# Pooling keys of batch 0 and values of batch 1 on TensorE, with the first zeroing on VectorE

## The chip, the cores and the metric

The kernel runs on one core of one Trainium2 chip. The time of a run is what the device takes from start to end, in microseconds (us). Five engines work side by side, each through its own instructions in order: TensorE (PE: matrix products and transposes), VectorE (DVE), ScalarE (ACT), GpSimd (POOL) and SyncE (SP), which here issues all transfers between the device's memory and the core's (DMA). An engine that waits for a result of another stands still, and all that is queued behind it waits too.

## What is computed

```python
def _attn_ref(q, k, v):                  # q, k, v: 8 x 8 x 576 x 64
    k_p = k.reshape(B, H, Sp, pool, D).mean(axis=3)     # pool = 8, Sp = 72
    v_p = v.reshape(B, H, Sp, pool, D).mean(axis=3)
    scores = scale * np.matmul(q, k_p.transpose(0, 1, 3, 2))
    attn = softmax(scores)
    return np.matmul(attn, v_p)
...
x = attn_out                             # 4608 tokens x 512
x = (relu(x @ w_in) ** 2) @ w_out        # 512 -> 2048 -> 512
out = (sigmoid(x @ w_gate) * (x @ w_val)) @ w_out2      # 512 -> 1536 -> 512
```

Each attention head looks at 72 pooled keys and values instead of 576. The two feed-forward layers that follow are nearly all of the arithmetic.

## The kernel before

The 4608 tokens are cut into 12 blocks of 384 (`NA`). A block goes through attention in two halves of four heads (`attend`), then through the first layer (`expert1`): for each of 16 slices f of the hidden width, twelve matmuls make h (line 818), ScalarE and VectorE make g = relu(h)^2 and split it into an upper and a lower part (`ghi`, `glo`, line 874), and twelve matmuls add g times `w_out` to the block's sums (line 827). The first block is done in two parts with the second between them, so that the weights are needed later. The second layer follows in a second stage, after about 980 us.

The products are made from two-part numbers: each weight and each activation is split into an upper part of short mantissa and the rest, and three of the four products are added. A weight must therefore be converted before its first use (`convert`, `split`): a transfer brings it into a raw tile, GpSimd adds a constant (`round24`, line 236), ScalarE takes the absolute value (line 242), VectorE does four steps (lines 246, 249, 252, 257), ScalarE makes the upper part (line 273) and VectorE the lower (line 277, into `in` or `out`). All 32 weight slices are converted while the first two blocks run.

Keys and values are pooled in two ways. On VectorE: a sum over eight neighbours (`tensor_reduce`), line 627 for the keys of batch 0, two heads at a time (`early_keys`), and line 379 for the others, head by head (`prep`). On TensorE: `early_kv` loads all heads of one batch in three transfers of 128, 128 and 32 partitions, each partition with two neighbouring rows, and multiplies by the matrix `pm`, whose ones add up the rows that belong together (`pool_rows`, line 659). ScalarE copies the sum out. For keys TensorE then transposes the heads in pairs (line 697), and ScalarE puts them into `kpT`, from which the scores are made (line 441). `early_kv` is used for the values of batch 0 and the keys of batch 1. `pm` is made on VectorE (lines 357, 358) from the identity `ident`, which GpSimd makes in `constants`; there GpSimd also zeroes the two `kpT` and two `e_sb` tiles (line 354).

The order of all this isn't written out. `Plan` holds every operation with its engine, an estimated duration in us, a rank (its due time), its dependences and the buffers that it takes and gives. `Plan.run` plays the program through with these durations: at each moment an engine that is free takes the operation of least rank among those that are ready and whose buffers are free. The sequence that comes out is the order in which each engine gets its instructions. So a changed duration or rank can change the order anywhere, and the engines then run that order, whatever the true durations are.

Of the kernel before, what the change touches and what calls it, by code (L numbers as in the profile page):

```python
# [131 lines left out]
def kernel(  # L132
# [53 lines left out]
    V0L = 1.0  # L186
# [8 lines left out]
    n = 0  # L195
# [31 lines left out]
    def convert(src, rank, at, get_raw, raw_name, get_t, t_name, done, load_rank=None):  # L227
# [37 lines left out]
        for fn, d in ((b1, 0.36), (b2, 0.36), (b3, 0.62)):  # L265
            o = op("dve", d, fn, (o,), rank)
        o = op("dve", 0.62, b4, (o,), rank, give=(raw_name,))
        return done(s, o)

    def split(s, o, rank, get_slot, take, give, key):  # L270
# [11 lines left out]
        return op("dve", 0.63, lo, (o,), rank, give=give)  # L282
# [68 lines left out]
    def constants():  # L351
        make_identity(nc, ident)
        for t in kpT + e_sb:
            nc.gpsimd.memset(t, 0.0)

    def constants2():
        nc.vector.memset(pm, 0.0)
# [13 lines left out]
    def prep(be, hf, rank):  # L371
# [24 lines left out]
        for pr in range(2 if be > 1 else 0):  # L396
            ds = []
            for j in range(2):
                h = 4 * hf + 2 * pr + j
                o = op("dma", 0.5, lambda h=h: load(k, h), rank=rank, at=rank - 20, take=("kv",), lag=2.0)  # L400
                ds.append(op("dve", 0.6, lambda pr=pr, j=j, h=h: red_k(pr, j, h), (o,) + tuple(ds), rank,
# [4 lines left out]
        for h in range(4 * hf, 4 * hf + 4):  # L406
# [8 lines left out]
            v_ready[be, h] = op("dve", 0.6, red_v, [o] + prev + first, rank + 3, give=("kv",))  # L415
# [143 lines left out]
    def attend(b, hf, rank, step, q_ops, fast, bank_of):  # L559
# [3 lines left out]
        for a in range(NTA):  # L563
# [28 lines left out]
            else:  # L592
                late.append(op("dve", 0.47, lambda a=a: a_trans(b, hf, a), [o] + late[-1:], r + 4,
# [22 lines left out]

    def early_keys(n, rank):
        tiles, st = {}, {}
        for i in range(KT):
            def ld(i=i):  # L620
                tiles[i] = t = wpool.tile([SP, 2, POOL, D], F32, tag=w1_tag(n + i), name="rows8")
                nc.sync.dma_start(
                    out=t, in_=k[0, 2 * i:2 * i + 2].rearrange("h (n r) d -> n h r d", r=POOL))

            def red(i=i):
                st[i] = att.tile([SP, 2, D], F32, tag="kp", name="kp", bufs=2)
                nc.vector.tensor_reduce(
                    out=st[i], in_=tiles[i].rearrange("n h r d -> n h d r"), op=ALU.add, axis=AX.X)

            def tr(i=i):  # L630
                st["ps", i] = p = ps("acc3", 1)
                nc.tensor.transpose(p[:, 0:SP], st[i].rearrange("n j d -> n (j d)"), ident[0:SP, 0:SP])

            def place(i=i):
                for j in range(2):
                    nc.scalar.activation(
                        out=kpT[0][64 * j:64 * j + 64, i, j * SP:(j + 1) * SP],
                        in_=st["ps", i][64 * j:64 * j + 64, 0:SP], func=ACTF.Copy)
# [148 lines left out]
    for hf in range(2):  # L787
        prep(1, hf, t1 - P1 + A1 * hf)
# [636 lines left out]
```

## Time and profile before

| what | us |
|---|---|
| median of 3 runs | 1813.4 (1811.69 to 1816.31) |
| the profiled execution | 1808.99 |
| its span, first to last instruction | 1807.2 |
| TensorE busy | 1750.7 (97%) |
| VectorE busy | 1167.3 (65%) |
| ScalarE busy | 774.9 (43%) |
| GpSimd busy | 243.9 (13%) |

The profile is of one execution, and all rows quoted here are of that one; it lies 4.4 us under the median. Busy shares are means over the whole span, in which the stages differ; a stage is read from its own stretch. Where a row ends in square brackets, they hold the time that the engine was idle before it and what ended the wait.

### The profile page before, as it was taken

Reading aid. Unit: us, or ns where it says so; the run is one execution under the profiler, and the core shown is the slowest. Engines: PE = TensorE matmul, PEld = TensorE weight load, DVE = VectorE, ACT = ScalarE, POOL = GpSimd, SP = SyncE. Lnnn points to the kernel's source line nnn. Section 1 sums busy time; section 2 is a strip of 40 time slices with the busy share of each in tenths; the row PEclk is TensorE's granted clock in tenths of the full one; section 3 lists DMA queues with packets and bytes.
Section 4 is the critical chain, followed back from the end, with each engine's and each line's share of the span. In section 5 each row is a group of like instructions: output and inputs, shape, how many; then the busy total and the mean of one; then the engine's idle time right before and its main releaser. Section 6 shows DMA issues by size and latency. Waiting matters only on the chain.

```text
span 1807.2 us, 26430 instructions
## 1 busy us (share of the span) xinstructions
PE 1750.7 (97%) x9696; PEld 1636.6 (91%) x9696; DVE 1167.3 (65%) x2318; ACT 774.9 (43%) x1722; POOL 243.9 (13%) x190
## 2 busy tenths in 40 slices
PE   5899999999999999999999999999999999999999
PEld 2688889999899888999999999999999999999998
DVE  6999787778767776664246555555655655655554
ACT  4766533333333333233245444444444444444442
POOL 3400000000000000000013211212111211211100
PEclk9999999999999999999999999999999999999999
DMA  9732344433343333320112222223433333333321
GB/s 246 238 94 71 82 110 106 123 105 102 91 99 102 113 99 98 81 79 24 52 53 94 70 71 70 82 71 105 132 99 113 114 108 114 109 106 105 105 80 50
DMA packets 191250, 179.15 MB, mean 99 GB/s; under 512 B 105232, under 2 KB 139024, under 8 KB 191120
## 3 DMA queue, kind: packets, MB, share of 16 engines
q1 hardware_dynamic: 191120, 177.46, 33.1%
q8 instruction: 76, 1.25, 0.3%
q14 instruction: 54, 0.44, 0.1%
HBM read 119.80 MB, written 48.76 MB: 93 GB/s over the span
## 4 chain that ended last, share of the span: by engine, by line
PE 61%; DVE 2%; SPq 1%; DMA 1%; issue 0%; ACT 0%; POOL 0%; DVEq 0%; POOLq 0%; ACTq 0%
PE h L1208 16%; PE acc L1323 16%; PE att L1208 8%; PE acc L827 8%; PE h L818 7%; PE acc L1208 4%; SPq L518 1%; PE att L542 0%; PE att L441 0%; DVE kp L379 0%; DVE g L874 0%; DMA aT<-T 0%; DMA raw<-in_moe_w_val_dram 0%; DMA kv<-in_k_dram 0%; DVE r L867 0%
## 5 line engine op out<-in xcount | busy, mean ns | idle before, releaser
L827 PE MATMUL acc<-g,out 128*128 128x384 f32 x2304 | 447.9, 340 | 17.4 <-DVE g L874 9.4
L818 PE MATMUL h<-x,in 128*128 128x384 f32 x2304 | 439.5, 339 | 2.3 <-DVE x L812 1.3
L827 PEld LDWEIGHTS acc<-g,out 128*128 128x128 f32 x2304 | 399.7, 188 | 39.5 <-DVE g L874 19.3
L818 PEld LDWEIGHTS h<-x,in 128*128 128x128 f32 x2304 | 403.0, 189 | 10.1 <-issue 6.2
L861 ACT ACTIVATE r<-h 128x384 f32<-128x384 f32 x192 | 93.8, 489 | 232.7 <-PE h L818 229.3
L1323 PE MATMUL acc<-in,p 128*128 128x512 f32 x648 | 182.5, 390 | 0.0
L1323 PE MATMUL acc<-out,p 128*128 128x512 f32 x648 | 182.1, 389 | 0.0
L1230 ACT ACTIVATE res<-h 128x384 f32<-128x384 f32 x144 | 70.6, 491 | 211.7 <-PE h L1208 210.9
L871 ACT ACTIVATE g<-r 128x384 fp32r<-128x384 f32 x192 | 100.8, 525 | 138.7 <-DVE r L867 131.4
L867 DVE TENSOR_TENSOR r<-r,h 128x384 f32<-128x384 f32 x160 | 87.7, 548 | 111.8 <-ACT r L861 111.6
L1323 PEld LDWEIGHTS acc<-out,p 128*128 128x128 f32 x648 | 121.7, 188 | 25.7
L874 DVE TENSOR_TENSOR g<-r,g 128x384 fp32r<-128x384 f32 x192 | 112.3, 585 | 50.4 <-ACT g L871 49.9
L1323 PEld LDWEIGHTS acc<-in,p 128*128 128x128 f32 x648 | 121.4, 188 | 24.1
L236 POOL INT64_ADD raw<-raw x40 | 43.7, 1092 | 658.5 <-DMA raw<-in_moe_w_out_dram 278.8
L1239 DVE TENSOR_TENSOR res<-res,acc 128x384 f32<-128x384 f32 x72 | 39.7, 551 | 125.3 <-PE acc L1208 125.3
L1349 DVE TENSOR_TENSOR o<-o,acc 128x512 f32<-128x512 f32 x72 | 49.5, 687 | 96.0 <-PE acc L1323 81.2
L1289 ACT ACTIVATE p<-res 128x384 fp32r<-128x384 f32 x144 | 75.3, 523 | 70.5 <-DVE res L1283 70.3
L1041 POOL TENSOR_TENSOR yt<-yf,yt 128x768 f32<-128x768 f32 x32 | 62.2, 1944 | 270.8 <-DVE out L1068 269.6
L1208 PE MATMUL h<-out,in 128*128 128x384 f32 x432 | 98.4, 335 | 0.0
L1208 PE MATMUL h<-in,out 128*128 128x384 f32 x432 | 98.1, 334 | 0.2 <-DVE res L1239 0.2
L1208 PE MATMUL h<-in,in 128*128 128x384 f32 x432 | 98.1, 334 | 0.0
L1208 PE MATMUL h<-out,out 128*128 128x384 f32 x432 | 98.0, 334 | 0.0
(146 smaller groups left out, 2646.2 us busy)
## 6 DMA issues: line engine op xcount, KB each, us to landing
yf<-y_dram SPq DMA_DIRECT2D x16, 1536.0 KB
o_part<-o SPq DMA_DIRECT2D x72, 256.0 KB
o<-o_part SPq DMA_DIRECT2D x72, 256.0 KB
y_dram<-y SPq DMA_DIRECT2D x48, 192.0 KB
w_dram<-t SPq DMA_DIRECT2D x36, 256.0 KB
w2s<-w_dram SPq DMA_DIRECT2D x36, 256.0 KB
out_dram<-o SPq DMA_DIRECT2D x36, 256.0 KB
kv<-in_v_dram SPq DMA_DIRECT2D x56, 144.0 KB
```

The lines of the kernel that those rows point to most:

```text
L818: nc.tensor.matmul(out=h[:, 0:n], lhsT=w[:, a, kk * 128:(kk + 1) * 128], rhs=xs[kk][:, c], start=(kk == 0 and i == 0), stop=(kk == KT - 1 ...
L827: nc.tensor.matmul(out=y_ps[m][:, 0:NA], lhsT=w[:, a, m * 128:(m + 1) * 128], rhs=g_t[f][:, c], start=(f == f0 and i == 0), stop=(f == f1 ...
L861: nc.scalar.activation(out=r, in_=st["h"][:, 0:NA], func=ACTF.Relu)
L867: nc.vector.tensor_tensor(out=st["r"], in0=st["r"], in1=st["h"][:, 0:NA], op=ALU.mult)
L871: nc.scalar.activation(out=g[:, 0], in_=st["r"], func=ACTF.Copy)
L874: nc.vector.tensor_tensor(out=g_t[f][:, 1], in0=st["r"], in1=g_t[f][:, 0].bitcast(F32), op=ALU.subtract)
L1041: nc.gpsimd.tensor_tensor(out=t, in0=q(a), in1=q(c), op=ALU.subtract)
L1208: nc.tensor.matmul(out=st[which, z][:, 0:HN], lhsT=w[:, wa, col:col + 128], rhs=ys[y, k2][:, yc], start=(first[z] == m and k2 == 0 and j = ...
L1230: nc.scalar.activation(out=new((which, key)), in_=st[which, z][:, 0:HN], func=ACTF.Copy)
L1289: nc.scalar.activation(out=p_t[fi][:, 0, h * HN:(h + 1) * HN], in_=st["gate", key], func=ACTF.Copy)
L1323: nc.tensor.matmul(out=o_ps[i], lhsT=p_t[f][:, a, i * 128:(i + 1) * 128], rhs=wslot[c, "out", f][:, w], start=(f == 0 and j == 0), stop=(f ...
L1349: nc.vector.tensor_tensor(out=st2["o"], in0=st2["o"], in1=o_ps[i], op=ALU.add)
```

## The change

Four things are changed.

- `early_keys` is gone. The keys of batch 0 go through `early_kv`, on TensorE, into the bank `acc3`. Their three transfers get a rank that places them ahead of the first two weights.
- The values of batch 1 go through `early_kv` too, where `prep` pooled them head by head on VectorE.
- The zeroing of `kpT` and `e_sb` goes from GpSimd to VectorE, as an operation of its own ahead of everything.
- The plan's durations for VectorE are longer: conversion steps, poolings, transposes and the lower parts of weights and g.

```diff
-    V0L = 1.0
+    V0L, V1L = 1.0, 4.0
...
-        for fn, d in ((b1, 0.36), (b2, 0.36), (b3, 0.62)):
+        for fn, d in ((b1, 0.4), (b2, 0.4), (b3, 0.66)):
...
-        o = op("dve", 0.62, b4, (o,), rank, give=(raw_name,))
+        o = op("dve", 0.66, b4, (o,), rank, give=(raw_name,))
...
-        return op("dve", 0.63, lo, (o,), rank, give=give)
+        return op("dve", 0.67, lo, (o,), rank, give=give)
...
     def constants():
         make_identity(nc, ident)
+
+    def zeros():
+        nc.vector.memset(pm, 0.0)
         for t in kpT + e_sb:
-            nc.gpsimd.memset(t, 0.0)
+            nc.vector.memset(t, 0.0)
 
     def constants2():
-        nc.vector.memset(pm, 0.0)
...
-                ds.append(op("dve", 0.6, lambda pr=pr, j=j, h=h: red_k(pr, j, h), (o,) + tuple(ds), rank,
+                ds.append(op("dve", 1.05, lambda pr=pr, j=j, h=h: red_k(pr, j, h), (o,) + tuple(ds), rank,
...
-            v_ready[be, h] = op("dve", 0.6, red_v, [o] + prev + first, rank + 3, give=("kv",))
+            v_ready[be, h] = op("dve", 1.05, red_v, [o] + prev + first, rank + 3, give=("kv",))
...
-                late.append(op("dve", 0.47, lambda a=a: a_trans(b, hf, a), [o] + late[-1:], r + 4,
+                late.append(op("dve", 0.56, lambda a=a: a_trans(b, hf, a), [o] + late[-1:], r + 4,
...
-    def early_keys(n, rank):
...
-    c1 = op("pool", 1.9, constants, rank=-10)
+    c1 = op("pool", 0.6, constants, rank=-10)
+    c0 = op("dve", 1.2, zeros, rank=-11)
     for n in range(2):
         convert_w1(n)
-    c2 = op("dve", 0.4, constants2, [c1], rank=-10)
-    early_keys(n1 - 8, 0.5)
+    c2 = op("dve", 0.4, constants2, [c1, c0], rank=-10)
+    early_kv(0, k, n1 - 8, -0.5, ("acc3", 1), [c2], True)
...
-    for hf in range(2):
-        prep(1, hf, t1 - P1 + A1 * hf)
+    early_kv(1, v, n1 - 11, t1 - P1 + V1L, K1B, [c2], False)
...
-            o = op("dve", 0.5, glo, [o], t - 50, give=("r",))
+            o = op("dve", 0.55, glo, [o], t - 50, give=("r",))
...
-                q_ops[a] = op("dve", 0.42, lambda a=a, hf=hf: q_trans(b, hf, a), loads + [q_ops[x] for x in q_ops], rank - 6 + a,
+                q_ops[a] = op("dve", 0.56, lambda a=a, hf=hf: q_trans(b, hf, a), loads + [q_ops[x] for x in q_ops], rank - 6 + a,
```

What this does to the order is shown at three places. Line numbers differ between the two kernels, since the program is shorter: lines 632, 670, 712, 443 and 791 of the changed one are lines 659, 697, 739, 441 and 818 of the one before.

TensorE at the start of the program, before: the pooled keys `kp` come from VectorE and are transposed one pair at a time (line 632), the queries `rows` are transposed (line 739), and the scores go to `att` and `h`.

```order
L632 MATMUL acc_122<-ident,kp 128x72
L632 MATMUL acc_128<-ident,kp 128x72
L739 MATMUL acc_135<-ident,rows_105 128x128 x2
L739 MATMUL acc_135<-ident,rows_114 128x128
L739 MATMUL acc_141<-ident,rows_105 128x128 x2
L739 MATMUL acc_141<-ident,rows_114 128x128
L441 MATMUL att<-kpT_78,qT_146 128x144 x2
L441 MATMUL h<-kpT_78,qT_146 128x144 x2
L632 MATMUL acc_161<-ident,kp 128x72
L441 MATMUL att<-kpT_78,qT_146 128x144 x2
L632 MATMUL acc_177<-ident,kp 128x72
```

And with the change, the same place:

```order
L632 MATMUL acc_104<-rows_95,pm 72x512 x2
L632 MATMUL acc_104<-rows_98,pm 72x512 x2
L632 MATMUL acc_104<-rows_100,pm 72x512 x2
L670 MATMUL acc_130<-ident,kp_124 128x72 x4
L712 MATMUL acc_140<-ident,rows_111 128x128 x2
L712 MATMUL acc_140<-ident,rows_116 128x128
L712 MATMUL acc_145<-ident,rows_111 128x128 x2
L712 MATMUL acc_145<-ident,rows_116 128x128
L443 MATMUL att<-kpT_78,qT_150 128x144 x2
L443 MATMUL h<-kpT_78,qT_150 128x144 x2
L443 MATMUL att<-kpT_78,qT_150 128x144 x2
```

Six pooling matmuls stand first, the four transposes follow in one piece, and nothing waits for VectorE between them and the scores.

VectorE at the start of the program, up to the first maximum of the scores (`m`), before:

```order
L357 MEMSET pm 128x160
L358 TENSOR_REDUCE pm<-ident 128x32
L246 TENSOR_SCALAR t_w<-t_w 128x512
L627 TENSOR_REDUCE kp<-rows_100 72x128
L627 TENSOR_REDUCE kp<-rows_103 72x128
L249 TENSOR_SCALAR t_w<-t_w 128x512
L246 TENSOR_SCALAR t_w<-t_w 128x512
L252 SCALAR_TENSOR_TENSOR t_w<-raw_w,t_w 128x512
L249 TENSOR_SCALAR t_w<-t_w 128x512
L627 TENSOR_REDUCE kp<-rows_118 72x128
L257 SCALAR_TENSOR_TENSOR t_w<-raw_w,t_w 128x512
L627 TENSOR_REDUCE kp<-rows_130 72x128
```

And with the change, from the first zeroed `kpT`:

```order
L357 MEMSET kpT_78 128x576
L357 MEMSET kpT_79 128x576
L357 MEMSET e_80 128x384
L357 MEMSET e_81 128x384
L360 TENSOR_REDUCE pm<-ident 128x32
L246 TENSOR_SCALAR t_w<-t_w 128x512
L249 TENSOR_SCALAR t_w<-t_w 128x512
L252 SCALAR_TENSOR_TENSOR t_w<-raw_w,t_w 128x512
L246 TENSOR_SCALAR t_w<-t_w 128x512
L257 SCALAR_TENSOR_TENSOR t_w<-raw_w,t_w 128x512
L249 TENSOR_SCALAR t_w<-t_w 128x512
L252 SCALAR_TENSOR_TENSOR t_w<-raw_w,t_w 128x512
```

Four zeroings have come in, the four poolings of keys are gone, and seven conversion steps stand ahead of the first maximum, which is the next row in both.

TensorE around the first matmuls of the first layer (`h<-x,in`), before; `kp` are the keys of batch 1, `vp` the values of batch 0:

```order
L818 MATMUL h<-x,in_168 128x384 x6
L697 MATMUL att<-ident,kp_414 128x72 x4
L542 MATMUL acc_431<-aT,vp 64x384 x2
L542 MATMUL acc_440<-aT,vp 64x384 x2
L739 MATMUL att<-ident,rows_325 128x128 x2
L739 MATMUL att<-ident,rows_434 128x128
L818 MATMUL h<-x,in_168 128x384 x3
```

And with the change:

```order
L791 MATMUL h<-x,in_155 128x384 x6
L670 MATMUL att<-ident,kp_402 128x72 x4
L544 MATMUL acc_420<-aT,vp 64x384 x2
L544 MATMUL acc_428<-aT,vp 64x384 x2
L632 MATMUL att<-rows_298,pm 72x512 x2
L791 MATMUL h<-x,in_155 128x384 x6
L632 MATMUL att<-rows_315,pm 72x512 x2
L632 MATMUL att<-rows_329,pm 72x512 x2
L712 MATMUL att<-ident,rows_360 128x128 x2
```

The pooling of the values of batch 1 has come in, its first two matmuls between the two halves of the first product and four behind it. In `early_kv` a batch after the first (`hold`) starts only when all three of its transfers have landed.

On SP the three transfers of the keys stand ahead of the first two weights, and those of batch 1's values directly behind the keys of batch 1, ahead of the third `out` weight; eight transfers of values that stood among later weights are gone.

## Rows read from the trace of the kernel before

**Rows 1.** Busy time by stretch: stretch, length, then engines, granted clock, DMA share, GB/s.

```profile
0.00:20.00 20.00, 2.24 (x9) 1.73 (x10) 6.70 (x10) 4.26 (x9) 4.50 (x12) 1.00 0.95 228
20.00:200.00 180.00, 158.51 (x861) 135.96 (x862) 174.73 (x342) 121.73 (x346) 38.37 (x30) 0.95 0.51 147
200.00:980.00 780.00, 766.85 (x4489) 727.69 (x4488) 530.22 (x1115) 282.70 (x593) 59.04 (x56) 1.00 0.33 88
980.00:1807.20 827.20, 823.11 (x4342) 771.19 (x4340) 455.69 (x854) 366.19 (x777) 142.02 (x93) 1.00 0.29 96
```

**Rows 2.** Waits of TensorE, 48 to 203 us: total us, times, longest.

```profile
PE att L526 <- DVE e L503: 3.7, 2, 3.5
PE acc L827 <- DVE out L277: 3.5, 2, 2.8
PE att L388 <- DVE kp L379: 2.2, 2, 1.9
PE acc L827 <- DVE g L874: 1.6, 3, 0.9
```

**Rows 3.** Groups of VectorE by line and shape, 0 to 200 us: busy us, mean ns.

```profile
L252 DVE SCALAR_TENSOR_TENSOR t_w<-raw_w,t_w 128x512 uint32<-128x512 uint32 x28 | 20.7, 746 | 0.2
L257 DVE SCALAR_TENSOR_TENSOR t_w<-raw_w,t_w 128x512 uint32<-128x512 uint32 x28 | 19.9, 715 | 0.0
L379 DVE TENSOR_REDUCE vp<-kv 72x64 f32<-72x512 f32 x16 | 16.7, 1072 | 0.0
L249 DVE TENSOR_SCALAR t_w<-t_w 128x512 uint32<-128x512 uint32 x32 | 16.3, 515 | 0.1
...
L246 DVE TENSOR_SCALAR t_w<-t_w 128x512 f32<-128x512 f32 x32 | 15.0, 478 | 12.7 <-ACT t_w L242 12.7
...
L627 DVE TENSOR_REDUCE kp<-rows 72x128 f32<-72x1024 f32 x4 | 7.5, 1884 | 0.0
```

**Rows 4.** Instructions in order of time, 0 to 30 us: start us, duration us.

```profile
0.83 0.19 DVE L357 MEMSET pm<- 128x160 f32 x1 [0.83 <-PEq L1409]
...
1.47 1.09 POOL L354 MEMSET kpT<- 128x576 f32 x2
...
2.50 0.78 POOL L354 MEMSET e<- 128x384 f32 x2
...
4.75 1.28 ACT L242 ACT_TABLE_LOAD   x1 [4.75 <-DMA raw_w<-in_moe_w_in_dram]
...
12.02 2.05 POOL L236 INT64_ADD raw_w<-raw_w  x2 [8.74 <-issue]
...
13.78 0.57 DVE L246 TENSOR_SCALAR t_w<-t_w 128x512 f32<-128x512 f32 x1 [11.95 <-ACT t_w L242]
...
16.30 0.35 PE L632 MATMUL acc<-ident,kp 72*128 72x72 f32 x1 [16.30 <-DVE kp L627]
...
19.75 1.40 PE L441 MATMUL att<-kpT,qT 128*128 128x144 f32 x4
...
23.72 0.44 DVE L484 TENSOR_REDUCE m<-att 128x4 f32<-128x288 f32 x1
...
23.94 0.26 PE L632 MATMUL acc<-ident,kp 72*128 72x72 f32 x1 [0.66 <-DVE kp L627]
...
24.75 5.52 PE L659 MATMUL acc<-rows,pm 128*72 128x512 f32 x12 [0.55 <-ACT kpT L636]
```

**Rows 5.** Busy time by stretch, as in the first group, of two shorter stretches.

```profile
39.00:43.00 4.00, 3.15 (x13) 1.10 (x10) 3.86 (x11) 3.48 (x16) 1.61 (x2) 1.00 0.10 19
...
80.00:100.00 20.00, 15.37 (x79) 12.17 (x80) 19.57 (x36) 10.91 (x32) 9.58 (x8) 0.74 0.62 203
```

**Rows 6.** Instructions in order of time: start us, duration us; three later places.

```profile
48.22 1.30 PE L818 MATMUL h<-x,in 128*128 128x384 f32 x6
...
199.29 0.55 DVE L874 TENSOR_TENSOR g<-r,g 128x384 fp32r<-128x384 f32 x1
...
261.72 0.25 PE L388 MATMUL att<-ident,kp 72*128 72x72 f32 x1 [1.45 <-DVE kp L379]
```

More of the change, by code (lines that the diff above doesn't have):

```diff
@@ L614, in attend @@
                                    [o], rank + 60, lag=2.0))
-    def early_keys(n, rank):
[L618 to L638, printed above, removed]
-            tag = w1_tag(n + i)
-            o = op("dma", 0.84, ld, rank=rank + (KH if i > 1 else 0.0) + 0.05 * i, take=(tag,), lag=2.0)
-            o = op("dve", 1.15, red, (o,), rank, take=("kp",), give=(tag,))
-            o = op("pe", 0.12, tr, (o, c1), rank, take=("acc3",), give=("kp",))
-            k_ready[0, i] = op("act", 0.5, place, (o,), rank, give=("acc3",))
     rows = [(0, 128), (128, 128), (256, S // 2 - 256)]
```

## Prediction

> **What bounds the kernel now.** First the busy time by stretch [rows 1]. Up to 20 us almost nothing runs. From 20 to 200 us VectorE is busy 174.73 of 180 us, so it never waits for long, while TensorE is busy 158.51 and idle 21.5. From 200 us on it is the other way round: TensorE is busy 98 to 99%, VectorE 68% and 55%. So the kernel is bound by TensorE nearly everywhere, by VectorE in the first 200 us, and by the first loads before 20 us. The waits of TensorE between the first expert matmul and 203 us [rows 2] say who starves it: its four longest rows, 11.0 us, all wait for a VectorE result: normalised e, a weight's lower half `out`, pooled keys, g. Next what VectorE spends its time on [rows 3]: four poolings of keys of batch 0 take 7.5 us; sixteen poolings of values take 16.7 us at 1072 ns, and eight of these are batch 1's. Last the start in order of time [rows 4]: GpSimd ends its zeroing at 3.28, its first `round24` begins at 12.02 after 8.74 us in which nothing is waited for, VectorE's first conversion step follows at 13.78, then the keys. The first scores run at 19.75, and the first maximum on VectorE at 23.72, since two more key poolings stand ahead of it.
>
> **What leaves VectorE.** Four key poolings, 7.5 us, and eight value poolings of batch 1, 8 x 1.072 = 8.6 us [rows 3]: together **16.1 us**, all from the stretch in which it is saturated. In the two orders I counted VectorE's instructions ahead of the 25th subtraction of g, which runs at 199.29 [rows 6]: the difference is these twelve, the zeroing, and the small steps of two softmax pieces that trade places (under 1 us net). The same count ahead of the 8th subtraction gives these twelve, the zeroing and two `x_lo`. So the gain is not put back by other work that is pulled forward.
>
> **What VectorE gets.** Zeroing of 2 x 576 + 2 x 384 columns. Its own zeroing of 160 columns takes 0.19 us [rows 4], so 1920 columns take 12 x 0.19 = 2.3 us, done by about 3.4. VectorE has nothing to do there before 13.78, and `pm` is ready before any key row can land. Cost nothing; if that cover were gone, 2.3 us.
>
> **GpSimd's start.** Without 1.9 us of zeroing (1.09 + 0.78) it is through at about 1.5, where its zeroing now begins. If the 8.74 us follow from there, the first `round24` starts at 10.3 and VectorE's conversions at 12.0, **1.8 us earlier**. If they end at a fixed time, 0. I take 1.8, because no row shows what else could hold it: the weight's first 512 KB had landed by 4.75, when the table load ran [rows 4]. In the changed kernel the keys (1.18 MB) go ahead of these weights. At 228 GB/s [rows 1] they take 5.2 us, so the first weight lands near 4.75 + 5.2 = 9.9, still ahead of 10.3, and the second 2.3 us later, near 12.2, about 0.9 us after GpSimd could take it.
>
> **The first scores.** VectorE's seven conversion steps ahead of the first maximum (4.2 us by the means in [rows 3]: two each of L246, L249 and L252, one of L257) would let it go at 16.2. But the keys now take another road: landing, 12 pooling records on TensorE (six matmuls of f32, two records each), ScalarE's copy, four transposes, two copies, then scores. The pooling is 5.52 us for a tensor at 25 us [rows 4]. Before that the transposes of keys took 0.35 us at 16.30 and 0.26 at 23.94 [rows 4], so the clock is likely at its lower level, 1.2 GHz, early on; the upper end for the pooling is therefore 11 us. With the first key tile near 4.75, the 11 us end at 15.8. From the first key transpose to the first scores the trace takes 3.4 us (16.30 to 19.75), so the first maximum comes at about 19.2. With 5.52 us the pooling is over early, and q, 0.39 MB behind the weights and so near 13.9, sets it at 13.9 + 3.4 = 17.3. I take 18.0, nearer to the second, since the pooling starts alone and the clock need not stay low. Against 16.2 that is a wait of 1.8 us on VectorE, bounds 1.1 to 3.0. It takes back the gain of GpSimd's start: **net 0**. The first maximum moves from 23.72 to 18.0, by 5.7 us.
> The Trainium skill, "TensorE: Matmul & The Clock Gate", section "What's actually happening", says that the clock is throttled by default and that activity releases it. That speaks against pooling on an engine that has just woken. Taken strictly, all twelve records run at 1.2 GHz, the wait is 3.0 and the sum below is 1.2 us worse; by a release halfway it is as I have it. No row of the kernel before has TensorE at work at 5 us.
>
> **Waits that appear.** VectorE idles 5.3 us in 20 to 200 [rows 1]. With 9% less to do it will stand more often behind ScalarE's exponentials and copies. I allow **+3.0 us**, a little over half of the present idle time again; bounds 0.5 and 5.5.
>
> **TensorE's added work.** 11.0 us of pooling; the keys' part runs in the empty start, and their transposes number four as before. Batch 1's 5.5 us stand in the queue between the halves of the first expert matmul, and everything behind waits for them. Can TensorE keep up with a VectorE that is 13 us faster? From the first expert matmul (48.22) to the 25th g (199.29) [rows 6] 151.1 us pass. With the start 5.7 us earlier it must save another 7.4 there and do 5.5 more: 12.9 us. It has the waits [rows 2], at least 11.0 us, and time at the lower clock: from 80 to 100 us a mean grant of 0.74 [rows 5], which loses 20 x 0.26 = 5.2 us. So it can, barely: VectorE and TensorE are then nearly in balance, which is why I do not take more.
>
> **The queues.** Values of batch 1 come as three transfers (1.18 MB) from SP ahead of the third `out` weight, instead of eight later ones of the same bytes. At 228 GB/s [rows 1] each load behind them lands 5.2 us later. What hides it: from 39 to 43 us the queues run empty, at 19 GB/s and a share of 0.10 [rows 5], so what was issued had landed and waited for VectorE. If that cover is gone, 5.2 us at worst.
>
> **After 200 us.** The longer VectorE times reorder small steps of later blocks. TensorE is idle 13 us in 200 to 980 [rows 1]. The key transposes stand equally far behind their poolings in both orders, but for the batches up to 262 us, one of which costs 1.45 [rows 6]. 0, with bounds of -3 and +3. After 980 us the order is the same.
>
> **Sum.** -16.1 + 0 + 3.0 = **-13.1 us**. The profiled execution took 1808.99 (span 1807.2), so it becomes 1795.9; the median shown lies 4.4 us above the profiled one, so I predict 1813.4 - 13.1 = **1800.3**.
>
> **Rivals.**
> - TensorE becomes the bound: only the earlier start and the two longest single waits (3.5 and 2.8 in [rows 2]) come back, less the pooling: -5.7 - 6.3 + 5.5 = -6.5, **1806.9**. For it: the balance above is tight. Against: the weights' conversions move forward among VectorE's rows, and the waits for `out` with them.
> - More comes back: VectorE's 16.1 and GpSimd's 1.8 in full, and the 5.2 us of the lower clock as TensorE is fed evenly: about -22 at the end, -18 for VectorE's part alone, **1795.4** down to 1791. Against: the scores' road.
> - It ends slower: TensorE stands at key transposes after 200 us, because the plan's longer times place a pooling behind the transpose that needs it. One such stall is 1.45 us at 261.72 [rows 6], 1.9 at most in [rows 2]; the order has eighteen transposes there, so 18 x 1.9 = 34, -13.1 + 34 = +21, **1834**. It decides from a mean stall of 0.73 us (13.1 / 18). Against: in the order most of them keep four or more expert groups between pooling and transpose.
> - It doesn't do what it says: the keys are no sooner there, since pooling at the low clock, copies and transposes eat the lead, and the first expert matmul stays near 48 us; then only the values' 8.6 less 5.5 count: -3.1, **1810.3**, no change.
>
> **How the numbers follow.** Forecast (between 1795.9 + 4.4 - 5 and + 5) 0.55; TensorE bound 0.17; more 0.15; no change 0.08; slower 0.05. The range takes the forecast, "more" to 1791 and "TensorE bound" with 3 us for the later blocks: 1791 to 1810. About 0.3% (5.4 us) is what a measurement of this kernel can tell from no change, so faster means below 1808.0: forecast, more, and two thirds of "TensorE bound" give 0.82; within 0.3% a third of that and the eighth part: 0.13; slower 0.05.
>
> **What would show it.** In the changed kernel: first `round24` near 10.3; first maximum near 18; first expert matmul near 42.5; the 25th subtraction of g near 186; TensorE's idle time in 20 to 190 us below 12 us and its 2.8 us wait for `out` gone; idle from 200 to 980 still near 13. It is wrong if the 25th g comes early and the end does not (then TensorE lost it later), or if the first maximum is later than 20.

## The result and the profile after

| what | before | after |
|---|---|---|
| median, us | 1812.55 | 1785.5 (1782.4 to 1788.42) |
| ratio | | 0.9842, interval 0.9823 to 0.986 |
| the profiled execution, us | 1808.99 | 1785.78 |
| its span, us | 1807.2 | 1784.0 |

The kernel became faster, by 27 us in the medians and 23.2 us in the spans. The forecast was 13.1 us, so the sign was right and the size about half, and the measured time lies below the range. The profiled execution of the kernel before lies 3.6 us under the median of this table and that of the changed kernel lies at its median, so what follows explains the 23.2 us of the spans; the rest of the 27 is spread of the runs. Lines that are named below: 791 (first matmuls of the first layer), 800 (second), 847 (g), 443 (scores) and 632 (pooling matmuls); in the kernel before they are 818, 827, 874, 441 and 659.

First the busy times by stretch in the changed kernel, in the columns of [rows 1]; the last two lines are the short stretches of [rows 5].

```profile
20.00:200.00 180.00, 162.29 (x890) 136.62 (x889) 169.53 (x331) 122.91 (x334) 40.09 (x30) 0.96 0.52 151
200.00:980.00 780.00, 776.71 (x4581) 745.00 (x4580) 539.54 (x1128) 291.18 (x611) 69.19 (x59) 1.00 0.33 90
...
39.00:43.00 4.00, 4.00 (x23) 2.22 (x22) 4.00 (x7) 3.69 (x9) 1.82 (x2) 1.00 1.06 306
80.00:100.00 20.00, 19.34 (x129) 17.34 (x128) 19.21 (x42) 16.76 (x46) 0.74 (x1) 1.00 0.17 34
```

The line to read is the second. TensorE was idle 13.15 of 780 us there [rows 1] and is now idle 3.29, with a granted clock of 1.00 in both kernels. The forecast had left this stretch at nothing. In 20 to 200 us the idle time fell only from 21.5 to 17.7.

The start in order of time, as in [rows 4], and two later places, as in [rows 6]: start, duration, engine, and in brackets the idle time before and what ended it.

```profile
5.10 7.98 PE L632 MATMUL acc<-rows,pm 128*72 128x512 f32 x12 [5.10 <-DMA rows<-in_k_dram]
...
9.15 1.03 POOL L236 INT64_ADD raw_w<-raw_w  x1 [7.65 <-DMA raw_w<-in_moe_w_in_dram]
...
13.86 0.45 PE L670 MATMUL acc<-ident,kp 72*128 72x72 f32 x4 [0.78 <-ACT kp L665]
...
15.73 0.90 PE L443 MATMUL att<-kpT,qT 128*128 128x144 f32 x4 [0.77 <-ACT qT L716]
...
16.66 0.46 DVE L486 TENSOR_REDUCE m<-att 128x4 f32<-128x288 f32 x1 [0.20 <-PE att L443]
...
38.88 1.29 PE L791 MATMUL h<-x,in 128*128 128x384 f32 x6
...
41.79 1.94 PE L632 MATMUL att<-rows,pm 128*72 128x512 f32 x4
...
191.83 0.56 DVE L847 TENSOR_TENSOR g<-r,g 128x384 fp32r<-128x384 f32 x1
```

The keys are pooled by 13.08, the first maximum moved from 23.72 to 16.66 and the first expert matmul from 48.22 to 38.88, a lead of 9.3 us. At the 25th subtraction of g the lead is 7.5 us (199.29 to 191.83). The span ends 23.2 us earlier. So two thirds of the gain were made after the place at which the forecast expected it to be complete. Following the second matmuls of each slice, of which 192 run before stage two, shows where:

| first matmul of line 827 / 800 in slice | before | after | lead |
|---|---|---|---|
| 5 | 91.6 | 85.5 | 6.0 |
| 8 | 113.7 | 100.2 | 13.5 |
| 25 | 202.9 | 195.8 | 7.1 |
| 33 | 237.9 | 230.9 | 6.9 |
| 97 | 551.2 | 532.8 | 18.4 |
| 145 | 778.4 | 755.3 | 23.2 |
| 192 | 984.6 | 961.4 | 23.2 |

From slice 33 to 145 before takes 540.5 us and after 524.4: 16.1 us, with the same instructions on TensorE in both. From there to the end nothing changes. This "late length" is what the experiments below compare.

The waits of TensorE, 230 to 740 us, before: total, times, longest.

```profile
PE acc L827 <- DVE g L874: 7.6, 16, 1.6
PE acc L827 <- ACT g L871: 3.0, 4, 1.2
PE att L388 <- DVE kp L379: 1.5, 1, 1.5
```

And after, the whole answer:

```profile
PE acc L800 <- DVE g L847: 2.3, 5, 0.7
PE acc L800 <- ACT g L844: 0.2, 1, 0.2
```

The 12.1 us became 2.5. That is less than the late gain, but the ends of matmuls are modelled in the profile, so idle time read from their rows can be too small. The weight loads for these matmuls, which overlap the matmuls, stood idle 26.7 us in this stretch before and 10.9 after (the number behind the second bar). That difference, 15.8, is about the late gain. Before:

```profile
L827 PEld LDWEIGHTS acc<-g,out 128*128 128x128 f32 x1260 | 217.7, 188 | 26.7 <-DVE g L874 14.9 <-ACT g L871 5.0 <-issue 4.5
```

After:

```profile
L800 PEld LDWEIGHTS acc<-g,out 128*128 128x128 f32 x1313 | 227.4, 188 | 10.9 <-DVE g L847 4.1 <-issue 3.0 <-ACT xf L552 2.4
```

What such a wait looks like, in the kernel before, VectorE and TensorE at slice 92 (start, duration):

```profile
523.81 1.11 DVE L379 TENSOR_REDUCE kp<-kv 72x64 f32<-72x512 f32 x1 [1.67 <-DMA kv<-in_k_dram]
525.80 1.01 DVE L379 TENSOR_REDUCE kp<-kv 72x64 f32<-72x512 f32 x1 [0.89 <-DMA kv<-in_k_dram]
526.74 0.54 DVE L874 TENSOR_TENSOR g<-r,g 128x384 fp32r<-128x384 f32 x1
...
527.34 2.20 PE L827 MATMUL acc<-g,out 128*128 128x384 f32 x11 [1.56 <-DVE g L874]
```

Two poolings of keys stand ahead of g in VectorE's row and wait for their transfers, 1.67 and 0.89 us; g and with it TensorE waits behind them. In the plan each of them was put down at 0.6 us; they take 1.0 to 1.1. This is the longest of the sixteen waits for g on VectorE. In seven of them, 3.9 of the 7.6 us, a pooling is among the four instructions ahead of g; in the other nine these are steps of the softmax, transposes and the like. So the poolings are about half of the story. In the changed kernel, the same slice:

```profile
509.07 1.06 DVE L381 TENSOR_REDUCE kp<-kv 72x64 f32<-72x512 f32 x1
510.05 0.54 DVE L847 TENSOR_TENSOR g<-r,g 128x384 fp32r<-128x384 f32 x1
...
511.12 1.07 DVE L381 TENSOR_REDUCE kp<-kv 72x64 f32<-72x512 f32 x1
...
510.96 2.24 PE L800 MATMUL acc<-g,out 128*128 128x384 f32 x12
```

Between two poolings there is now a g, the transfers have landed, and TensorE's row is without a gap. Summed over 230 to 740 us, VectorE's waits for work that is not the slice's own, and first that for `r`, which is, before:

```profile
DVE r L867 <- ACT r L861: 33.1, 30, 2.6
...
DVE t L246 <- ACT t L242: 15.4, 11, 4.0
DVE T L509 <- DMA aT<-T: 9.0, 8, 2.1
DVE kp L379 <- DMA kv<-in_k_dram: 8.1, 6, 2.1
DVE vp L379 <- DMA kv<-in_v_dram: 3.6, 2, 1.8
```

And after:

```profile
DVE r L840 <- ACT r L834: 56.7, 43, 5.2
...
DVE kp L381 <- DMA kv<-in_k_dram: 5.3, 5, 2.9
DVE t L246 <- ACT t L242: 5.0, 3, 2.5
DVE T L511 <- DMA aT<-T: 3.8, 4, 1.1
```

Without `r`, 36.1 us became 14.4, counting 0.3 for `vp` that the lines leave out. The wait for `r`, which follows from TensorE's own h, grew from 33.1 to 56.7: VectorE is more often ahead of TensorE instead of holding it up.

### The profile page after: what moved, and what is told of

Read it like the earlier page. It is cut to its first block, busy times and chain, and to the rows that moved or that the text cites. A ratio compares the mean times of both kernels' runs of the same rounds, so it can differ in the third digit from the quotient of the medians.

```text
span 1784.0 us, 26488 instructions
## 1 busy us (share of the span) xinstructions
PE 1752.6 (98%) x9720; PEld 1636.1 (92%) x9720; DVE 1160.5 (65%) x2310; ACT 774.6 (43%) x1718; POOL 245.9 (14%) x186
## 4 chain that ended last, share of the span: by engine, by line
PE 89%; DVE 3%; ACT 1%; DMA 1%; issue 1%; SPq 1%; POOL 0%; DVEq 0%; ACTq 0%; POOLq 0%
PE acc L800 20%; PE h L791 19%; PE h L1181 17%; PE acc L1296 17%; PE att L1181 8%; PE acc L1181 4%; PE att L544 2%; PE att L443 2%; DVE g L847 0%; DMA kv<-in_k_dram 0%; POOL raw L236 0%; SPq L427 0%; DVE kp L381 0%; DMA raw<-in_moe_w_out_dram 0%; DVE vp L381 0%
## 5 line engine op out<-in xcount | busy, mean ns | idle before, releaser
L800 PE MATMUL acc<-g,out 128*128 128x384 f32 x2304 | 439.3, 338 | 5.1 <-DVE g L847 2.5
```

The costliest lines, as they stand in the source:

```text
L800: nc.tensor.matmul(out=y_ps[m][:, 0:NA], lhsT=w[:, a, m * 128:(m + 1) * 128], rhs=g_t[f][:, c], start=(f == f0 and i == 0), stop=(f == f1 ...
```

## The experiments

The question after the result: does the late gain of 16 us come from the durations in the plan, which is the theory, or from the moved work and its earlier lead, which is the rival? And what is each part worth? The span and the two parts of it, up to slice 33 and from 33 to 145, are from one profiled execution each; the medians and ratios (to the kernel before on the same chip) from timed runs. Timed runs of one kernel lie 3 to 11 us apart here, so a difference of a few us between two spans or late lengths settles nothing by itself.

| kernel | median | ratio, interval | span | slice 33 at | late length |
|---|---|---|---|---|---|
| before | 1812.55 | 1 | 1807.2 | 237.9 | 540.5 |
| after | 1785.5 | 0.9842, 0.9823 to 0.986 | 1784.0 | 230.9 | 524.4 |
| e1_old_times | 1796.9 | 0.9937, 0.9915 to 0.9959 | 1794.7 | 229.7 | 536.0 |
| e2_times_only | 1800.52 | 0.9942, 0.9924 to 0.9959 | 1799.7 | 245.3 | 525.7 |
| e3_values_on_vector | 1795.94 | 0.9915, 0.9898 to 0.9931 | 1794.9 | 238.8 | 527.3 |
| e4_keys_on_vector | 1793.75 | 0.9905, 0.9887 to 0.9923 | 1792.7 | 244.3 | 519.9 |
| e5_pool_times | 1793.04 | 0.9879, 0.9846 to 0.9912 | 1790.0 | 232.6 | 531.0 |
| e6_trans_times | 1798.21 | 0.9907, 0.9877 to 0.9936 | 1797.4 | 229.5 | 541.0 |
| e7_g_times | 1801.23 | 0.9924, 0.9896 to 0.9951 | 1795.3 | 229.4 | 537.3 |
| e8_conv_times | 1798.43 | 0.9901, 0.987 to 0.9932 | 1797.8 | 226.8 | 542.4 |
| f1_pool_old | 1793.12 | 0.9896, 0.9878 to 0.9913 | 1790.7 | 230.3 | 533.8 |
| f2_zero_gpsimd | 1785.24 | 0.9851, 0.9837 to 0.9866 | 1783.6 | 232.1 | 522.7 |
| f3_truer_times | 1788.91 | 0.9873, 0.9856 to 0.989 | 1787.3 | 235.4 | 523.8 |
| f4_no_round | 1766.3 | 0.9745, 0.9729 to 0.976 | 1766.5 | 215.4 | 522.6 |
| g1_new_late | 1784.13 | 0.984, 0.9825 to 0.9854 | 1783.3 | 229.2 | 525.5 |
| g2_new_early | 1797.94 | 0.991, 0.9891 to 0.9929 | 1799.1 | 230.3 | 540.3 |

**The moves without the durations, and the durations without the moves.** e1_old_times is the changed kernel with every VectorE duration of the plan as before:

```diff
-        for fn, d in ((b1, 0.4), (b2, 0.4), (b3, 0.66)):
+        for fn, d in ((b1, 0.36), (b2, 0.36), (b3, 0.62)):
...
-            v_ready[be, h] = op("dve", 1.05, red_v, [o] + prev + first, rank + 3, give=("kv",))
+            v_ready[be, h] = op("dve", 0.6, red_v, [o] + prev + first, rank + 3, give=("kv",))
...
-            o = op("dve", 0.55, glo, [o], t - 50, give=("r",))
+            o = op("dve", 0.5, glo, [o], t - 50, give=("r",))
```

> The changed kernel with the plan's old VectorE durations; pooling, zeroing and loads stay moved. Theory A (the longer durations in the plan brought the larger part, between 230 and 740 us, where TensorE's waits for g went from 11 to 2.5 us): about 15 us of the 27 are lost again, 1800, and TensorE waits for g in the later blocks as in the kernel before. Theory B (the moved work brought it all, the durations nothing, as predicted): 1786, within 3 us of the changed kernel.

e2_times_only is the kernel before with the same lines changed the other way round, and nothing else.

> The kernel before with the new VectorE durations in the plan and nothing else. Theory A: about 15 us faster than before, 1797, with the waits for g between 230 and 740 us under 4 us. Theory B: 1812, within 3 us of before.

With the old durations the moves give 12.5 us of span, 8.2 of them by slice 33: about the 13.1 of the forecast. The durations alone give 7.5, but as a loss of 7.4 by slice 33 and a gain of 14.8 behind it. With the new durations the moves give 15.7 (1799.7 to 1784.0), of which 14.4 by slice 33. So nearly all of the late gain belongs to the durations, whatever was moved; e1's late length is 4.5 us under that of before, which is within the spread. That the 12.5 comes near the forecast is partly luck, since the forecast had its 13.1 in the first 200 us. Both kernels came out between the two theories, nearer to the one that gave the larger part to the durations. The idle time of the weight loads, 230 to 740 us, says the same. e1_old_times:

```profile
L800 PEld LDWEIGHTS acc<-g,out 128*128 128x128 f32 x1273 | 220.3, 188 | 21.7 <-DVE g L847 9.5 <-ACT g L844 6.0 <-issue 4.1
```

e2_times_only:

```profile
L827 PEld LDWEIGHTS acc<-g,out 128*128 128x128 f32 x1296 | 224.4, 188 | 12.0 <-DVE g L874 4.3 <-ACT xf L550 3.5 <-issue 3.3
```

The early loss of e2 shows in part in TensorE's waits for weights, 20 to 230 us. The kernel before has 3.5 us for the lower part of `out` [rows 2]; e2 has 3.9 for its upper part and 3.5 for `in`:

```profile
PE acc L827 <- ACT out L273: 3.9, 2, 2.2
...
PE h L818 <- DVE in L277: 3.5, 5, 1.3
```

**Each move undone.** e3_values_on_vector pools batch 1's values on VectorE again:

```diff
-    early_kv(1, v, n1 - 11, t1 - P1 + V1L, K1B, [c2], False)
+    for hf in range(2):
+        prep(1, hf, t1 - P1 + A1 * hf)
```

> The changed kernel with the values of batch 1 pooled on VectorE again. Theory A1 (VectorE is the bound there, 8.6 us of poolings come back and 5.5 us of TensorE work goes): 3 us slower than the changed kernel, 1788.5. Theory B1 (TensorE's pooling in the middle of the first products costs as much as it frees, since the gain shrinks from 9 to -1 us between 39 and 62 us): same or up to 4 us faster, 1782 to 1786.

e4_keys_on_vector brings `early_keys` back, behind the first weights:

```diff
-    early_kv(0, k, n1 - 8, -0.5, ("acc3", 1), [c2], True)
+    early_keys(n1 - 8, 0.5)
```

> The changed kernel with the keys of batch 0 pooled on VectorE again, loaded behind the first weights. Theory A2 (the earlier start is kept to the end): 6 to 8 us slower than the changed kernel, 1792 to 1794. Theory B2 (the earlier start is lost again before 62 us, whatever it was): within 2 us of the changed kernel, 1784 to 1788.

Undoing the values' move costs 10.9 us of span (1794.9 against 1784.0), where the expectation was 3 or nothing; undoing the keys' costs 8.7. The VectorE time that the moves free is 8.6 and 7.5 [rows 3]. The two are not separate shares: together they make 19.6, and both moves at once gave 15.7. By slice 33 they cost 7.9 and 13.4, and behind it 2.9 more and 4.5 less. TensorE's clock has a part in this: its mean grant in 20 to 200 us is 0.92 in e3 and 0.94 in e4 against 0.96, and 0.04 of 180 us is 7.2 us, an upper estimate for e3. What can be said is that each move pays, and that the 5.7 us that TensorE spends on batch 1's values (1.94 + 3.74, from 41.79 and 46.71 us) cost nothing that shows.

**Which durations.** Four kernels put one kind of new duration into e1: e5_pool_times the poolings (1.05), e6_trans_times the transposes (0.56), e7_g_times g (0.55), e8_conv_times the conversions. One, f1_pool_old, takes the poolings out of the full set:

```diff
-            v_ready[be, h] = op("dve", 1.05, red_v, [o] + prev + first, rank + 3, give=("kv",))
+            v_ready[be, h] = op("dve", 0.6, red_v, [o] + prev + first, rank + 3, give=("kv",))
```

> The moved work with, of the new VectorE times, only those of the poolings (0.6 to 1.05) in the plan. The whole set brings 11 us over the old times at the end. Theory A (the gain follows the time by which the plan was short: 96 poolings x 0.45 = 43 us of some 70 between 230 and 980 us): 1789 to 1791, most of the gain, all of it after 230 us. Theory B (what counts is the time of the g that TensorE waits for, not that of the poolings): 1797.

> The moved work with only the new times of the transposes (0.47 and 0.42 to 0.56). Theory A (short by 60 x 0.09 + 60 x 0.14 = 14 us): 1794 to 1795, 2 us under the old times. Theory B: 1797.

> The moved work with only the new time of g's lower part (0.5 to 0.55). Theory A (short by 160 x 0.05 = 8 us): 1795 to 1796, at most 2 us under the old times. Theory B (TensorE's waits for g in the later blocks go with this entry): 1788 to 1790.

> The moved work with only the new times of the conversion steps. Theory A: in the first 230 us, where 32 conversions run, the order gets worse or stays (the new times alone put the 33rd slice 7 us later there), after it 36 conversions x 0.2 = 7 us are corrected: 1795 to 1800. Theory B: 1797.

> The changed kernel with only the poolings' times set back to 0.6. Alone, the poolings' new times brought 4.7 us of span, the three other groups nothing or a loss. Theory A (the set works through the poolings, the rest is along for the ride): 1792 to 1796, 7 to 10 us slower than the changed kernel, with waits for g back after 230 us. Theory C (no single entry matters; each change of the table is a new draw of the order): anywhere from 1785 to 1797.

The poolings are the largest entry: alone they take 5.0 us off e1's late length, and without them the full set loses 9.4. The others bring no gain alone (541.0, 537.3 and 542.4 against 536.0). But 5.0 is not 11.6, the difference of e1 and the changed kernel: the rest came only with all entries together. So the expectation that each entry brings what it was short by did not hold: the poolings brought less than half of the gain, and the transposes and g nothing. Whether transposes and conversions alone make the late part longer, by 5.0 and 6.4 us, is not shown: it is one execution each, and the ratios of these two kernels are not above that of e1. One entry moves many rows of the order at once.

Is the gain then only a lucky draw of an order, the rival that f1 names? Not for the table as a whole. The eight kernels with the full set of new durations for the late operations (after, e2, e3, e4, f2, f3, f4 and g1 below, which lacks one entry of it) have late lengths of 519.9 to 527.3 us, the three without it (before, e1 and g2 below, which has that one entry) 536.0 to 540.5, though their early orders differ. For single entries the rival is not excluded.

**Early or late operations.** It could still be that new durations help by what they do to the first 230 us, with an echo later. g1_new_late has the old durations for the conversions of the first layer's weights, for the lower part of every weight and for g in the first three parts, and the new ones for the rest; g2_new_early the reverse.

```diff
+        conv_n.append(0)
+        x = 0.0 if len(conv_n) <= 32 else 0.04
-        for fn, d in ((b1, 0.4), (b2, 0.4), (b3, 0.66)):
+        for fn, d in ((b1, 0.36 + x), (b2, 0.36 + x), (b3, 0.62 + x)):
...
-            o = op("dve", 0.55, glo, [o], t - 50, give=("r",))
+            o = op("dve", 0.5 if i < 3 else 0.55, glo, [o], t - 50, give=("r",))
```

> The changed kernel with the new VectorE times only where they belong to later work: poolings and transposes of batches 2 and on, conversions of the second layer's weights, g from the fourth part on. First-layer weights and the g of the first three parts keep the old times. Theory E (the late gain comes from the times of the late operations): from the 33rd to the 145th slice 520 to 528 us, as with the whole new table, and the end at 1782 to 1787. Rival (it comes from the state in which the early part leaves the plan): 534 to 542 us there, as with the old table, end near 1796.

> The reverse: new times only for the first-layer weights and the g of the first three parts, old times for all later operations. Theory E: 534 to 542 us from the 33rd to the 145th slice, end at 1795 to 1800. Rival: 520 to 528 us, end near 1785.

Both reach slice 33 at the same time (229.2 and 230.3) and end 15.8 us apart. The durations of the late operations make the late gain, and those of the early ones gain nothing that shows. The same row as above, of line 804 here, g1_new_late:

```profile
L804 PEld LDWEIGHTS acc<-g,out 128*128 128x128 f32 x1303 | 225.8, 188 | 7.5 <-issue 3.6 <-DVE g L851 1.8 <-ACT xf L556 1.2
```

g2_new_early:

```profile
L804 PEld LDWEIGHTS acc<-g,out 128*128 128x128 f32 x1262 | 218.2, 188 | 24.9 <-DVE g L851 11.7 <-ACT g L848 6.8 <-issue 4.1
```

**More durations nearer to the trace.** f3_truer_times lengthens the softmax steps, `x_lo`, the square and the copies too:

```diff
-                o = op("dve", 0.78, lambda a=a: softmax3_few(b, hf, a), [o], r + 3)
+                o = op("dve", 0.9, lambda a=a: softmax3_few(b, hf, a), [o], r + 3)
...
-                o = op("dve", 0.5, sq, [o], t - 50, give=("h",))
+                o = op("dve", 0.55, sq, [o], t - 50, give=("h",))
```

> The changed kernel with the VectorE times that are still short made true as well: softmax, square, lower part of x, copies of sums. Theory A (the plan's order gets better as its VectorE times get true): waits of TensorE after 230 us go further down, 1780 to 1784. Theory C (each table is a new draw): 1780 to 1797, with no tie to the truth of the times.

No gain, where theory A expected 1.5 to 5.5 us: the late length stays (523.8), and slice 33 comes 4.5 us later. What was left to gain behind it was 3.3 us of idle time in TensorE's row. So longer entries that are nearer to the trace are not always better.

**The zeroing.** f2_zero_gpsimd puts the zeroing back on GpSimd:

```diff
+        for t in kpT + e_sb:
+            nc.gpsimd.memset(t, 0.0)
...
-        for t in kpT + e_sb:
-            nc.vector.memset(t, 0.0)
```

> The changed kernel with the zeroing of kpT and e_sb on GpSimd again. As predicted: first add on GpSimd 1.8 us later (near 11.0), the first maximum no later than 18, the end 0 to 2 us later, 1785 to 1787. Rival (the start is carried to the end in full): 3 us later, 1788.5.

GpSimd's first add is 1.95 us later (11.10 instead of 9.15), the first maximum at 16.8 instead of 16.7, and the end the same (span 0.4 less). This part of the change is worth nothing that shows, as forecast: in the changed kernel the first scores set the maximum.

**GpSimd's adds.** f4_no_round leaves GpSimd's rounding add out for all weights but the first two, so the weights' numbers are others; the rest of the conversion stays.

```diff
-            nc.gpsimd.int64_add(raw, raw, ROUND_AND_REBIAS)
+            rounds.append(1)
+            if len(rounds) < 3:
+                nc.gpsimd.int64_add(raw, raw, ROUND_AND_REBIAS)
```

> The changed kernel with GpSimd's add left out for all weights but the first two of the first layer, so the weights are not rounded and the numbers are others. Theory D (GpSimd at work stretches VectorE's operations, 0.68 to 1.52 us, some 23 us in the first 240 us, and this took part of the gain between 39 and 62 us): VectorE's operations at 40 to 80 us are at their short times, and the span is 8 to 15 us under the changed kernel, 1770 to 1777. Rival (the stretched operations are hidden): within 3 us, 1782 to 1787.

17.5 us less span, more than the 8 to 15 expected, 15.5 of them by slice 33; the late length is the same. What the adds do to VectorE stands in the last section. The 17.5 are an upper bound for that, as far as one run can give it: the step also leaves the chain of each conversion, and TensorE's granted clock in this stretch is higher, 0.99 against 0.96, which is 5.4 of 180 us at most. Its busy time in 20 to 200 us:

```profile
20.00:200.00 180.00, 172.28 (x981) 148.10 (x980) 158.25 (x356) 128.48 (x346) 0.00 (x0) 0.99 0.55 158
```

TensorE is idle 7.7 us there against 17.7 with the adds.

## Why the prediction was right and wrong

**The step that failed is "After 200 us".** It was put at 0 with bounds of -3 and +3, and it measures -14.8 by the durations alone (e2 against before, slices 33 to 145) and -16.1 in the changed kernel. I read TensorE's 13 us of idle time there, saw in the order that key transposes stood no nearer to their poolings, and stopped. I did not ask what the 13 us were made of. The trace of before had the answer: sixteen waits for g behind VectorE's row, 7.6 us, and 26.7 us of idle weight loads. A plan that is told 0.6 for a pooling of 1.07 us [rows 3] promises g too early, and that was the term to price: an upper bound of 26.7 from that row, not 3.

**A second miss, the other way: the lead at the 25th g.** The sum has its 13.1 us there, and the lead is 7.5. Had the rest been right, the change would have brought less than forecast; the two misses offset each other in part. VectorE's busy time (third pair of numbers) up to this g, before:

```profile
20.00:199.29 179.29, 157.81 (x857) 135.25 (x857) 174.05 (x339) 121.61 (x345) 38.37 (x30) 0.95 0.51 147
```

And after:

```profile
0.00:20.00 20.00, 13.35 (x43) 5.80 (x44) 9.43 (x24) 7.92 (x26) 2.86 (x9) 1.00 1.03 254
20.00:191.83 171.83, 154.12 (x844) 130.15 (x843) 162.56 (x313) 117.40 (x322) 40.09 (x30) 0.96 0.53 151
```

With the 6.70 before 20 us [rows 1] the busy time falls from 180.8 to 172.0, by 8.8 us. Of the 16.1 that left, 1.9 came back as zeroing, and 5.4 were lost because other instructions became longer, a term that the sum does not have (last section). VectorE's idle time fell by 2.7 before 20 us and rose by 4.0 after it. 8.8 and 2.7 less 4.0 is the 7.5. The sum also has no term for what the new durations do to the order of the first 200 us: alone they cost 7.4 us by slice 33 (e2), with the moves 1.2 (e1 against the changed kernel).

**What leaves VectorE: 16.1.** In the end it came back nearly whole: 15.7 us of span with the new durations, 12.5 with the old. VectorE's busy time over the whole span shrank less, from 1167.3 to 1160.5 or by 6.8, where 16.1 less 1.9 of zeroing would be 14.2; other instructions became longer (last section).

**GpSimd's start and the first scores: net 0.** Right at the end, by f2, and nearly right in its times: first add 9.15 (forecast 10.3), first maximum 16.66 (18.0). The wait of 1.8 us on VectorE ahead of the maximum is 0.20: its seven steps ran from 11.08 to 16.46, 5.4 us and not 4.2, with a wait of 1.1 for ScalarE among them. The pooling took 7.98 us, between my 5.52 and 11: the weight loads of its records start 0.85 us apart up to 9.41, and the last two, at 11.64 and 12.07, 0.43 apart, half speed and then full.

```profile
8.56 0.24 PEld L632 LDWEIGHTS acc<-rows,pm 128*72 128x72 f32 x1 [0.61 <-issue]
9.41 0.24 PEld L632 LDWEIGHTS acc<-rows,pm 128*72 128x72 f32 x1 [0.61 <-issue]
...
12.07 0.14 PEld L632 LDWEIGHTS acc<-rows,pm 32*72 32x72 f32 x1 [0.29 <-issue]
```

The granted clock is put down as 1.00 for this stretch, but the spacing says that it began at the lower of its two levels. The road from the first key transpose to the scores was then 1.9 us, not 3.4. By the rule cited there from the Trainium skill ("TensorE: Matmul & The Clock Gate", "What's actually happening") the clock starts low; the trace agrees for the first half, and it cost the maximum at most the 0.20 us of its wait.

**Waits that appear: +3.0.** Right in size: VectorE's idle time from 20 us to the 25th g rose by 4.0, within the bounds. Against e2, which has the same durations and 10.5 us of such idle time, it did not rise, and there the moves bring 15.7 of 16.1. TensorE's waits, 20 to 230 us, changed names more than size: 20.3 us in all before and 17.6 after. The longest four now:

```profile
PE h L791 <- DVE x L785: 3.0, 2, 1.8
PE att L443 <- ACT qT L716: 2.9, 1, 2.9
PE h L791 <- DVE in L277: 2.1, 3, 1.0
PE h L791 <- ACT in L273: 2.1, 2, 1.5
...
PE acc L800 <- DVE out L277: 0.3, 1, 0.3
```

The wait for `out` is gone as forecast, and waits for `in` took its place.

**TensorE in balance.** From the first expert matmul to the 25th g the forecast was 143.5 us, before had 151.1, after has 153.0. So TensorE saved nothing there; the lead at the 25th g is what the earlier start gave, 9.3 us, less 1.9. The values' pooling on TensorE is not the reason, since with them on VectorE (e3) slice 33 comes 7.9 us later still. The sign "TensorE idle below 12 us in 20 to 190" failed: it is idle 17.7 there.

**The queues: hidden.** The cover was gone. From 39 to 43 us the queues now run at 306 GB/s where they stood at 19 [rows 5], and GpSimd's adds 7 to 11 come 1.5 to 5.2 us later than before (the seventh at 34.36 instead of 32.89, the eleventh at 44.64 instead of 39.45) though all else is earlier. In e3, without the values' transfers ahead, the seventh add starts at 30.29 and the eleventh at 37.93, 4.1 and 6.7 us sooner, so the delay goes with them. How much of the lead this cost was not measured apart from the adds' own effect.

**The rivals.** "More comes back" names a number near the measured one (-22), but by another road: VectorE's time, GpSimd's and the clock, all before the 25th g. Only 7.5 us are there, so the nearness is luck (and its terms, 16.1, 1.8 and 5.2, add up to 23.1). The clock did rise in 80 to 100 us, from 0.74 to 1.00, but over 20 to 200 us only from 0.95 to 0.96. "Slower by key transposes" had the place right and the sign wrong: the longer times reordered the late blocks, and for the better. TensorE as the bound has the early part nearly right in number (-6.5, where the lead is 7.5), but not in kind: in f4, with VectorE's instructions shorter and the adds gone, slice 33 comes another 15.5 us earlier. "Does not do what it says" did not happen. (A slip in the chances: two thirds of 0.17 make 0.81 for faster and 0.14 for no change.)

## What to carry to other kernels

In a kernel whose order comes from a plan, compare each duration of the plan with its mean in the trace first, above all for operations that share an in-order engine with the critical ones: here entries that were up to 44% short cost 14.8 us, nearly as much as the 16.1 us of work that was moved. It is the whole set that counted, and still longer entries brought nothing more, so a table of durations has to be measured like any other change. A stretch that is 98% busy still has a price; look up what its idle time waits for before writing a zero. Taking work from a saturated engine paid here though the receiving engine was busy 88%: 16 us freed, 15.7 gained with the same durations in the plan, 12.5 with the old ones. But part of the freed time was lost to instructions that became longer, so look at what runs in its place.

## What the runs showed of the hardware

VectorE's instructions become longer while GpSimd's adds run. The changed kernel, VectorE and GpSimd around 61 us:

```profile
60.21 2.81 POOL L236 INT64_ADD raw_w<-raw_w  x2 [0.54 <-DMA raw_w<-in_moe_w_in_dram]
...
60.74 1.39 DVE L847 TENSOR_TENSOR g<-r,g 128x384 fp32r<-128x384 f32 x1
62.05 1.25 DVE L249 TENSOR_SCALAR t_w<-t_w 128x512 uint32<-128x512 uint32 x1
```

Undisturbed, g takes 0.55 us and the shift of line 249 takes 0.42. An add alone takes 1.04, and two of them take 2.81 here. The mean of that shift at 40 to 80 us (second number behind the first bar, ns), before:

```profile
L249 DVE TENSOR_SCALAR t_w<-t_w 128x512 uint32<-128x512 uint32 x6 | 3.3, 559 | 0.0
```

After:

```profile
L249 DVE TENSOR_SCALAR t_w<-t_w 128x512 uint32<-128x512 uint32 x7 | 5.4, 778 | 0.0
```

Without the adds, f4_no_round, where the line is 252:

```profile
L252 DVE TENSOR_SCALAR t_w<-t_w 128x512 uint32<-128x512 uint32 x10 | 4.2, 421 | 0.0
```

Counting every VectorE instruction up to 240 us that lasts over 0.25 us longer than the median of its form, the excess is 17.8 us before, 23.2 after and 0 without adds; each such instruction of either kernel overlaps an add. At 40 to 80 us it is 5.3 before and 14.6 after, mostly because 19 adds start in that stretch instead of 10, and there the lead of 9.3 us at 39 us shrinks to 4.3 at the first `acc` matmul (57.9 and 53.6). The value poolings that stood there before were not stretched: 1072 ns is their mean [rows 3], as later in the kernel (1.07 at 511 us). The Trainium skill ("SBUF — State Buffer", "Who interferes with whom") says that VectorE, in part of its instructions, and GpSimd share a pair of ports under an exclusive lock that one instruction holds to its end. The rows agree so far as the added time goes up to 0.84 us, less than one add, and each lengthened instruction overlaps one. Up to 240 us the kernels with adds have 33 or 34 of them, and yet their excess falls into two groups: 17.8 to 18.9 us in the three that pool batch 1's values on VectorE (before, e2 and e3), 21.6 to 24.8 in the twelve others. So it seems that with the poolings gone, conversion steps stood in their place that collide with the adds, and that part of the freed time was lost to them. No run separates this from the adds' own place in the chain.

The gap between GpSimd's set-up and its first add, 8.74 us in [rows 4], was 7.82 with the zeroing on GpSimd in f2 and 8.97 without it in f4. In the three kernels whose set-up ends at 3.28 (before, e2, f2) the first add starts at 11.10 to 12.69, in the thirteen where it ends at 1.51 at 9.04 to 11.09. So it comes later after a later set-up, but the gap varies by two microseconds, and in ten of the thirteen the profile puts its end down to the weight's transfer.
